# Summing six first-layer tiles of the last chunk in narrower column strips

## The chip, the cores and the metric

The kernel runs on one core of a Trainium2 chip. The metric is the device time of one execution in microseconds (us). Three executions of the kernel before took 631.61, 632.38 and 633.06 us, so its time is the median, 632.38 us. A further execution was recorded by the hardware profiler, and every duration below is read from that recording.

The profile's names for the engines are: PE is the matrix engine, PEld its loads of stationary operands (weights), DVE the vector engine, ACT the scalar engine, POOL the general-purpose engine and SP the engine that issues the transfers (DMA).

## The reference, cut to what matters

The program is an attention layer (local window plus block summaries) followed by two matrix products with a piecewise function between them. Only the second half is touched by the change:

```python
h = x @ w_in                      # x: 3072 x 512, w_in: 512 x 2048
neg = h <= -1.0
pos = h >= 1.0
g = np.where(pos, h, np.where(neg, 0.0, (h + 1.0) ** 2 / 4.0))
out = g @ w_out                   # w_out: 2048 x 512
```

Here `x` is the output of the attention, 4 x 768 tokens of 512 features.

## The kernel before

The 3072 tokens are worked through in eight chunks of 384 (`NCH` = 8, `T` = 384). A chunk c runs through the attention, whose result is written, transposed, into four pairs of tiles `xhi`, `xlo` (`xs[c, k]`, k = 0 to 3, 128 features by 384 tokens each), and then through the two layers.

Every float32 factor of the two layers is kept as a rounded part and a rest, both of the type float32r, and each product is made as three: weight rest times high, weight high times rest, and high times high. The weights (`halves`) are converted once, in the opening, and stay on the chip.

**The first layer**, `ff1` (line 422), makes one tile of `h` for each f = 0 to 15: 128 columns of `w_in` by the chunk's 384 tokens, summed over k = 0 to 3. That is 4 x 3 = 12 matmuls into one PSUM bank, each with a 128 x 128 block of weights as the stationary operand and 384 columns moving (line 426). The first of the twelve has `start`, the last has `stop`. A bank holds 512 columns; `h` uses 384 of them, and two banks take turns (`ps_h`, two buffers).

**The gate** turns `h` into `ghi` and `glo` in five steps on other engines: half (ACT, line 439), square (ACT, 442), minimum (DVE, 445, the last reader of `h`), rounding (ACT, 450), rest (POOL, 455).

**The second layer**, `ff2` (line 457), takes tile f of the gate's output as stationary and 512 columns of `w_out` as moving operand: 3 row blocks x 3 products = 9 matmuls with 512 columns each (line 464), summed over all f into three banks `acc`.

The order of the instructions on each engine is written out by hand as a text of steps: `OPENING` for chunk 0, `SECOND` for chunk 1, `LATER` for the rest. A step is a letter and its arguments: `F.d2` is `ff1` of the present chunk for f = 13 and k = 2, `B.b` is `ff2` for f = 11, `G`, `H`, `I`, `J`, `O` are the five gate steps. In `LATER` the four steps of a tile stand side by side, and the second layer follows two tiles behind:

```python
F.c0 F.c1 F.c2 F.c3 J.b O.b t+32 t+33 B.a G.c H.c u*0 F.d0 F.d1
F.d2 F.d3 I.c z*0 J.c u*1 O.c B.b G.d H.d z*1 I.d F.e0 ...
```

So on PE the last chunk (c = 7, which has no later chunk's attention beside it) is a plain alternation: twelve matmuls of tile f, nine of tile f - 2, twelve of tile f + 1, and so on.

`idle_products` (line 429, steps `j`) multiplies zeros by zeros, 128 x 128 by 128 columns of plain float32, in the opening while PE has nothing else to do. They matter below because they are the only other matmuls with whole 128 x 128 weights and few moving columns.

Of the kernel before, what the change touches and what calls it, by code (L numbers as in the profile page):

```python
# [19 lines left out]
P = 128  # L20
# [11 lines left out]
NCH = B * NHALF  # L32
NK = DM // P
NF = DFF // P
NTT = T // P
W_BUFS = 3
LAG = 2
E_BUFS = 2
OPENING = """
# [56 lines left out]
def fused_kernel(ctx: ExitStack, tc: tile.TileContext, q2, kT, kwin, vT, vwin, w_in, w_out, mask, ident, out):  # L96
    nc = tc.nc
# [24 lines left out]
    weight, raws, converting, joined, halves = {}, {}, {}, {}, {}  # L122

    def room(i, what, shape, dtype):

        return wpool.tile(shape, dtype, tag=f"w{i}", name=f"{what}{i}")
# [25 lines left out]
    def convert_join(i, n):  # L152
# [7 lines left out]
        else:  # L160
            if i not in converting:
                converting[i] = stage.tile([P, 2 * DM], I32, tag="w", name=f"w{i}", bufs=W_BUFS)
            nc.vector.scalar_tensor_tensor(out=converting[i][:, cols], in0=top[:, cols], scalar=-0x80000000, in1=joined[i, part],  # L163
# [15 lines left out]
    q_ts, k_ts, v_ts, s_pss, es, dens, t_pss, pts, vs_pss, o_pss, xs = ({} for _ in range(11))  # L179

    def input_tile(pool, what, shape, c, p):
        if c == 0 and (what, p) in at_first:
            return at_first[what, p]
        tag, bufs = ("w", W_BUFS) if pool is stage else (what, 2)
        return pool.tile(shape, F32, tag=tag, name=f"{what}{c}_{p}", bufs=bufs)
# [3 lines left out]
    for i, share in enumerate(FIRST):  # L189
        at, at_room = 0, room(NF - 1 - i, "first", [P, 4 * DM], F32)  # L190
# [227 lines left out]

    hs, ts, gs, acc, outs = {}, {}, {}, {}, {}

    def ff1(c, f, k):
        if k == 0:
            hs[c, f] = ps_h.tile([P, 512], F32, tag="h", name=f"h{c}_{f}")
        x_hi, x_lo = xs[c, k]
        for n, (w, x) in enumerate(((1, x_hi), (0, x_lo), (0, x_hi))):
            nc.tensor.matmul(hs[c, f][:, :T], weight["win", f][w][:, k * P:(k + 1) * P], x,  # L426
                             start=(k == 0 and n == 0), stop=(k == NK - 1 and n == 2))
# [39 lines left out]
    def result(c, i):  # L467
        o_sb = stage.tile([P, DM], F32, tag="w", name=f"o{c}_{i}", bufs=W_BUFS)
        if i == 1:
            nc.vector.tensor_copy(out=o_sb, in_=acc[c][i])  # L470
        else:
            nc.scalar.copy(out=o_sb, in_=acc[c][i])
        outs[c, i] = o_sb
# [5 lines left out]
    def load_constants(n):  # L479
# [13 lines left out]
        "p": values_of_two, "u": sum_vals_ahead, "z": turn_sums, "x": spread_sums, "L": low,  # L493
        "a": convert_top, "b": convert_low, "c": convert_join, "d": convert_high, "e": convert_rest,
        "F": ff1, "G": gate_half, "H": gate_square, "I": gate_min, "J": gate_high, "O": gate_rest, "B": ff2, "U": result, "o": store, "j": idle_products,
    }
    done = set()
# [92 lines left out]
```

## Time and profile before

| What | Value |
|---|---|
| median of three executions | 632.38 us |
| the profiled execution's own time | 632.96 us |
| its span, first to last instruction | 631.2 us |
| PE busy | 617.1 us, 98% of the span, 4388 matmuls |
| PEld busy | 550.4 us, 87%, 4388 loads |
| DVE, ACT, POOL busy | 57%, 53%, 41% |
| share of the first layer (line 426) in the chain that ended last | 41% |
| share of the second layer (line 464) in it | 42% |
| mean granted PE clock | 0.990 |

The profiled execution took 1.76 us more than its span, which is what lies before the first and after the last instruction. "Busy" for PE means that some matmul was under way; matmuls overlap, so the distance from the start of one to the start of the next says more than the duration of one. PEld is a row of its own because the weights of one matmul are loaded while the matmul ahead of it still runs.

### The profile page before, as it was taken

What the parts mean: (1) busy time and instruction counts of PE and PEld (TensorE: products, weight loads), DVE (VectorE), ACT (ScalarE), POOL (GpSimd) and SP (SyncE); (2) the same over time, 40 slices, a digit from 0 to 9 for tenths busy, and PEclk for the clock granted to TensorE, in tenths of its full rate; (3) what the DMA queues carried; (4) which work ended last, traced back from release to release, by engine and by line L of the source; (5) the groups of instructions that cost most, each with busy time, mean ns of one, the idle gap of its engine ahead of it and who ended that gap; (6) DMA issues with size and microseconds to landing.
All of it is one profiled execution on the core that took longest, in us unless ns stands there. A gap on an engine that the chain in (4) does not pass through costs nothing.

```text
span 631.2 us, 11762 instructions
## 1 busy us (share of the span) xinstructions
PE 617.1 (98%) x4388; PEld 550.4 (87%) x4388; DVE 357.8 (57%) x822; ACT 336.7 (53%) x877; POOL 259.4 (41%) x272
## 2 busy tenths in 40 slices
PE   8689999999999999999999999999999999999997
PEld 7578888898988989898898989889898988999995
DVE  5879787377836549376643737469363726411111
ACT  2679998454547353463635436373543636343342
POOL 2578999533533333333423434333332333212221
PEclk9879999999999999999999999999999999999999
DMA  8999953181124150251213033162202210010001
GB/s 305 299 309 359 275 178 80 54 247 46 52 64 123 51 158 4 78 182 38 74 38 99 25 103 109 38 196 65 73 1 82 79 38 2 1 50 1 2 0 51
DMA packets 49770, 63.57 MB, mean 101 GB/s; under 512 B 24881, under 2 KB 33329, under 8 KB 49713
## 3 DMA queue, kind: packets, MB, share of 16 engines
q1 hardware_dynamic: 49712, 62.81, 33.5%
q8 instruction: 35, 0.57, 0.4%
q14 instruction: 23, 0.18, 0.1%
HBM read 56.51 MB, written 6.29 MB: 99 GB/s over the span
## 4 chain that ended last, share of the span: by engine, by line
PE 91%; DMA 4%; POOL 2%; DVE 1%; ACT 1%; SPq 0%; issue 0%; POOLq 0%; ACTq 0%
PE acc L464 42%; PE h L426 41%; PE o_ps L415 3%; PE s_ps L360 3%; DMA raw<-in_w_in 2%; DMA raw<-in_w_out 1%; POOL halves L175 1%; PE o_ps L332 1%; PE t_ps L320 1%; DMA first<-in_kT 1%; PE h_idle L434 0%; PE s_ps L286 0%; DVE w L163 0%; POOL e L315 0%; DVE c L158 0%
## 5 line engine op out<-in xcount | busy, mean ns | idle before, releaser
L426 PE MATMUL h<-xhi,halves 128*128 128x384 f32 x1024 | 284.7, 339 | 2.8 <-POOL halves L175 1.8
L464 PE MATMUL acc<-halves,ghi 128*128 128x512 f32 x768 | 240.4, 394 | 0.0
L455 POOL TENSOR_TENSOR glo<-t,ghi 128x384 fp32r<-128x384 f32 x128 | 129.7, 1015 | 263.7 <-ACT ghi L450 186.8
L426 PEld LDWEIGHTS h<-xhi,halves 128*128 128x128 f32 x1024 | 187.3, 188 | 9.4 <-POOL halves L175 2.7
L445 DVE SCALAR_TENSOR_TENSOR t<-h,t 128x384 f32<-128x384 f32 x128 | 70.7, 556 | 205.1 <-ACT t L442 200.4
L426 PE MATMUL h<-xlo,halves 128*128 128x384 f32 x512 | 172.0, 336 | 0.0
L464 PEld LDWEIGHTS acc<-halves,ghi 128*128 128x128 f32 x768 | 144.1, 188 | 27.8
L464 PE MATMUL acc<-halves,glo 128*128 128x512 f32 x384 | 152.4, 397 | 0.0
L439 ACT ACTIVATE t<-h,ones_half 128x384 f32<-128x384 f32 x128 | 74.0, 579 | 131.9 <-PE h L426 122.6
L405 DVE STREAM_TRANSPOSE turned_blocks<-e 32x192 f32<-32x192 f32 x288 | 106.5, 370 | 20.5 <-POOL e L393 16.4
L450 ACT CAST ghi<-t 128x384 fp32r<-128x384 f32 x128 | 65.2, 511 | 96.5 <-DVE t L445 94.8
L426 PEld LDWEIGHTS h<-xlo,halves 128*128 128x128 f32 x512 | 96.3, 188 | 4.9
L464 PEld LDWEIGHTS acc<-halves,glo 128*128 128x128 f32 x384 | 72.1, 188 | 14.5 <-issue 2.1
L381 ACT ACTIVATE e<-e,den 128x120 f32<-128x120 f32 x144 | 55.2, 386 | 26.5 <-DVE den L375 26.5
L442 ACT ACTIVATE t<-t 128x384 f32<-128x384 f32 x128 | 66.6, 522 | 2.9
L393 POOL TENSOR_TENSOR e<-e,den 128x720 f32<-128x720 f32 x24 | 33.4, 1391 | 51.0 <-DVE den L387 23.7
L175 POOL TENSOR_TENSOR halves<-w,halves 128x1024 fp32r<-128x1024 f32 x16 | 38.6, 2412 | 5.4 <-DMA q<-in_q 4.2
L381 ACT ACTIVATION_READ_ACCUMULATOR e<-e,den 128x1 f32 x144 | 27.3, 189 | 0.0
L158 DVE SCALAR_TENSOR_TENSOR c<-raw,c 128x512 int32<-128x512 int32 x32 | 22.0, 690 | 6.3 <-ACT raw L144 3.0
L368 DVE SCALAR_TENSOR_TENSOR e<-s_ps,mask_sb 128x360 f32<-128x360 f32 x48 | 22.4, 523 | 5.6 <-PE s_ps L360 5.6
L304 ACT ACTIVATE e<-e,den 128x120 f32<-128x120 f32 x48 | 18.3, 384 | 10.2 <-DVE den L299 10.2
L150 ACT ACTIVATE c<-raw 128x512 int32<-128x512 uint32 x32 | 19.8, 627 | 5.8 <-DMA raw<-in_w_in 4.8
(77 smaller groups left out, 422.3 us busy)
## 6 DMA issues: line engine op xcount, KB each, us to landing
k<-in_kwin SPq DMA_DIRECT2D x28, 360.0 KB, 4.4
v<-in_vwin SPq DMA_DIRECT2D x30, 288.0 KB, 3.4
raw<-in_w_in SPq DMA_DIRECT2D x16, 512.0 KB, 10.1
raw<-in_w_out SPq DMA_DIRECT2D x16, 512.0 KB, 10.1
out<-o SPq DMA_DIRECT2D x24, 256.0 KB, 2.3
q<-in_q SPq DMA_DIRECT2D x56, 96.0 KB, 4.0
kraw<-in_kT SPq DMA_DIRECT2D x13, 384.0 KB, 4.2
vraw<-in_vT SPq DMA_DIRECT2D x13, 384.0 KB, 5.3
```

Of the source, the lines that this page charges most:

```text
L175: nc.gpsimd.tensor_tensor(out=lo, in0=converting[i].bitcast(F32), in1=hi.bitcast(F32), op=ALU.subtract)
L368: nc.vector.scalar_tensor_tensor(out=es[c, h][:, b, j], in0=s_pss[c, p, j][:, :NT * KA].rearrange("p (t n) -> p t n", n=KA), scalar=1.0 / ...
L381: nc.scalar.activation(out=e, in_=e, func=AF.Exp, bias=dens[c, p][:, 0, j, t:t + 1], scale=1.0, accum_out=dens[c, p][:, 1, j, t:t + 1])
L393: nc.gpsimd.tensor_tensor(out=e, in0=e, in1=den.unsqueeze(2).broadcast_to([P, 2 * NT, KA]), op=ALU.mult)
L405: nc.vector.transpose(out=pt[kb * SB:(kb + 1) * SB, :, qb * SB:(qb + 1) * SB], in_=e[qb * SB:(qb + 1) * SB, :, at:at + SB])
L426: nc.tensor.matmul(hs[c, f][:, :T], weight["win", f][w][:, k * P:(k + 1) * P], x, start=(k == 0 and n == 0), stop=(k == NK - 1 and n == 2))
L439: nc.scalar.activation(out=ts[c, f], in_=hs[c, f][:, :T], func=AF.Relu, bias=ones_half, scale=0.5)
L442: nc.scalar.square(out=ts[c, f], in_=ts[c, f])
L445: nc.vector.scalar_tensor_tensor(out=ts[c, f], in0=hs[c, f][:, :T], scalar=1.0, in1=ts[c, f], op0=ALU.max, op1=ALU.min)
L450: nc.scalar.copy(out=hi, in_=ts[c, f])
L455: nc.gpsimd.tensor_tensor(out=lo, in0=ts[c, f], in1=hi.bitcast(F32), op=ALU.subtract)
L464: nc.tensor.matmul(acc[c][i], a[:, rows], weight["wout", f][w], start=(f == 0 and n == 0), stop=(f == NF - 1 and n == 2))
```

## The change

The six tiles f = 4, 5, 8, 9, 12 and 13 of the last chunk are summed strip by strip: a new table gives the widths, and a new function runs the whole sum over k for the first strip of columns, then for the next. A strip has its own `start` and `stop`. All of it is issued in the step for k = 3; the steps for k = 0 to 2 of these tiles issue nothing. The columns computed, the order of the twelve terms of each sum, the bank and the gate's instructions stay as they are. The other ten tiles of the last chunk, and all other chunks, are not touched.

```diff
+STRIPS = {4: (192, 192), 5: (192, 192), 8: (256, 128), 9: (256, 128), 12: (128, 256), 13: (128, 128, 128)}
...
+    def ff1_in_strips(c, f):
+
+        at = 0
+        for width in STRIPS[f]:
+            cols = slice(at, at + width)
+            at += width
+            for k in range(NK):
+                x_hi, x_lo = xs[c, k]
+                for n, (w, x) in enumerate(((1, x_hi), (0, x_lo), (0, x_hi))):
+                    nc.tensor.matmul(hs[c, f][:, cols], weight["win", f][w][:, k * P:(k + 1) * P], x[:, cols],
+                                     start=(k == 0 and n == 0), stop=(k == NK - 1 and n == 2))
+
     def ff1(c, f, k):
         if k == 0:
             hs[c, f] = ps_h.tile([P, 512], F32, tag="h", name=f"h{c}_{f}")
+        if c == NCH - 1 and f in STRIPS:
+            if k == NK - 1:
+                ff1_in_strips(c, f)
+            return
         x_hi, x_lo = xs[c, k]
```

Each matmul brings a load of its 128 x 128 weights with it, so a strip of the same tile loads the same twelve blocks again. Two strips make 24 pairs of load and matmul where there were 12, three strips make 36: 5 x 12 + 24 = 84 pairs more in all.

The program's order on PE shows it. The names are tile, chunk and f (`h7_5` is tile f = 5 of chunk 7), then what moves and the weights; the last entry is partitions by moving columns. Before, the end of tile 5 and the start of the second layer that follows it:

```order
L426 MATMUL h7_5_6344<-xlo7_2_6133,halves4_727 128x384
L426 MATMUL h7_5_6344<-xhi7_2_6132,halves4_727 128x384
L426 MATMUL h7_5_6344<-xhi7_3_6144,halves4_727 128x384
L426 MATMUL h7_5_6344<-xlo7_3_6145,halves4_727 128x384
L426 MATMUL h7_5_6344<-xhi7_3_6144,halves4_727 128x384
L464 MATMUL acc7_0_6264<-halves4_727,glo7_3_6325 128x512
```

With the change, the same place in tile 5, where its first strip ends and its second begins:

```order
L431 MATMUL h7_5_6356<-xlo7_2_6133,halves4_727 128x192
L431 MATMUL h7_5_6356<-xhi7_2_6132,halves4_727 128x192
L431 MATMUL h7_5_6356<-xhi7_3_6144,halves4_727 128x192
L431 MATMUL h7_5_6356<-xlo7_3_6145,halves4_727 128x192
L431 MATMUL h7_5_6356<-xhi7_3_6144,halves4_727 128x192
L431 MATMUL h7_5_6356<-xhi7_0_5773,halves4_727 128x192
L431 MATMUL h7_5_6356<-xlo7_0_5774,halves4_727 128x192
```

Where the second layer stood next, the sum over k begins anew on the other 192 columns; the second layer's nine follow twelve matmuls later. The same seam in tile 13, with three strips of 128:

```order
L431 MATMUL h7_13_6640<-xhi7_3_6144,halves12_1193 128x128
L431 MATMUL h7_13_6640<-xlo7_3_6145,halves12_1193 128x128
L431 MATMUL h7_13_6640<-xhi7_3_6144,halves12_1193 128x128
L431 MATMUL h7_13_6640<-xhi7_0_5773,halves12_1193 128x128
L431 MATMUL h7_13_6640<-xlo7_0_5774,halves12_1193 128x128
```

Nothing moved past anything else: the order on DVE, ACT, POOL and SP has the same rows as before, and on PE only these six tiles have other rows.

## The prediction

> **What bounds the kernel now.** I read the chain that ended last first, since only what lies on it can move the end. In order of time, its last pieces (start, length, what) are these:
>
> ```profile
> 574.41 2.08 PE acc L464 x9
> 576.49 2.10 PE h L426 x12
> 578.59 2.08 PE acc L464 x9
> ...
> 605.80 2.10 PE h L426 x12
> 607.90 2.08 PE acc L464 x9
> 609.98 2.10 PE h L426 x12
> 612.09 2.08 PE acc L464 x9
> 614.17 2.10 PE h L426 x12
> 616.27 2.08 PE acc L464 x9
> 618.36 2.10 PE h L426 x12
> 620.46 6.18 PE acc L464 x27
> 626.64 0.02 issue
> 626.66 0.58 ACT o L472
> ```
>
> The last chunk is an unbroken alternation on PE, with no other engine in it until the final copy. The tiles follow each other every 4.19 us and the last, f = 15, starts at 618.36, so the rows at 576.49, 605.80 and 609.98 are f = 5, 12 and 13. Twelve first-layer matmuls take 2.10 us, **175 ns** a pair of load and matmul; nine second-layer ones take 2.08 us, **231 ns**. Next I asked whether PE pauses anywhere in that stretch (columns: window, its length, then busy time of the engines, the granted clock, DMA):
>
> ```profile
> core 0: us, PE busy (x) PEld busy (x) DVE busy (x) ACT busy (x) POOL busy (x), PEclk, DMA share, GB/s
> 572.30:618.36 46.06, 46.06 (x233) 41.73 (x232) 6.13 (x11) 17.82 (x34) 11.08 (x11) 1.00 0.00 1
> ```
>
> It doesn't: PE is busy for 46.06 of 46.06 us at full clock, and transfers are absent. So whatever a pair costs more goes straight to the end, unless another engine's slack has to be reckoned with. It is wide. Tile 12 ends as its second-layer neighbour starts, at 607.90, and its gate then runs as follows:
>
> ```profile
> 608.00 0.58 ACT L439 ACTIVATE t<-h,ones_half 128x384 f32<-128x384 f32 x1 [1.84 <-PE h L426]
> ...
> 609.24 0.56 DVE L445 SCALAR_TENSOR_TENSOR t<-h,t 128x384 f32<-128x384 f32 x1 [3.63 <-ACT t L442]
> ...
> 610.42 1.01 POOL L455 TENSOR_TENSOR glo<-t,ghi 128x384 fp32r<-128x384 f32 x1 [3.18 <-ACT ghi L450]
> ```
>
> `glo` is ready at 611.43 and PE first wants it two tiles later, at 616.27, so 4.8 us are spare; the bank is free at 609.80 and wanted by tile 14 at 614.17. Longer tiles only widen both. The change is therefore a pure question of PE: what does a pair with 192, 256 or 128 moving columns cost?
>
> **The price of a pair.** Two things can set it. The first is the streaming of the columns. Through 175 ns at 384 columns and 231 ns at 512 runs a line of 56 ns per 128 columns, which gives 119 ns at 256, 91 ns at 192 and 63 ns at 128. The second is the load of the weights. At 178.7 us a first-layer tile follows other work whose array layout is different, and its first load finds no cover (PE rows, then PEld rows):
>
> ```profile
> 178.72 0.44 PE L426 MATMUL h<-xhi,halves 128*128 128x384 f32 x1
> 178.99 0.34 PE L426 MATMUL h<-xlo,halves 128*128 128x384 f32 x1
> 179.17 0.52 PE L426 MATMUL h<-xhi,halves 128*128 128x384 f32 x2
> ```
>
> ```profile
> 178.71 0.19 PEld L426 LDWEIGHTS h<-xhi,halves 128*128 128x128 f32 x1
> 178.82 0.19 PEld L426 LDWEIGHTS h<-xlo,halves 128*128 128x128 f32 x1
> 179.00 0.36 PEld L426 LDWEIGHTS h<-xhi,halves 128*128 128x128 f32 x2
> ```
>
> Read the starts. Elsewhere a load starts as the matmul ahead starts (178.99 and 179.00 are such a pair): only one set of weights can wait behind the set in use. The first matmul is recorded at 178.72, but the next load starts at 178.82, as the columns of the first begin to stream; and the first matmul's record lasts 0.44 us where its neighbour's lasts 0.34. Both say that an uncovered load costs **0.10 to 0.11 us**, although its own record is 0.19 long. Hence the shortest possible rhythm: the matmul starts, the next load starts, 0.11 us later the next matmul starts, however few columns it has. That is a floor which 384 columns (175 ns) hide and 128 do not. One stretch of the opening shows loads at this rhythm, the products of zeros with 128 columns:
>
> ```profile
> 9.48 3.84 PE L434 MATMUL h_idle<-zeros 128*128 128x128 f32 x32
> ...
> 9.48 3.65 PEld L434 LDWEIGHTS h_idle<-zeros 128*128 128x128 f32 x32 [0.16 <-issue]
> ```
>
> From the first to the last load are 3.65 - 0.19 = 3.46 us for 31 steps, **112 ns** each. These are float32, whose columns may stream more slowly, so 112 ns is an upper bound for the load alone; with the 0.10 to 0.11 us from the other side I take 112 ns as the floor. Its ends are 105 ns (the load alone) and 119 ns (what 256 columns cost, the nearest price above).
>
> **The sum.** Pairs with 256 columns are set by streaming (119 ns), those with 192 and 128 by the floor (112 ns):
>
> - f = 4 and 5: 24 x 112 = 2.69 us for 2.10, +0.59 each, **+1.18**
> - f = 8, 9 and 12: 12 x 119 + 12 x 112 = 2.77 for 2.10, +0.67 each, **+2.02**; whether the wide strip comes first makes no difference, as each strip is twelve equal pairs
> - f = 13: 36 x 112 = 4.03 for 2.10, **+1.93**
>
> Together **+5.1 us**. Nothing covers it, and nothing is removed: the seam between two strips is one more pair of the same kind, since the array layout stays the same, and the second `start` waits for nothing, as the operands were ready before the tile began. With the floor at 105 ns the 120 narrow pairs (48 + 36 + 36) give 0.8 less, at 119 ns 0.8 more: +4.3 to +6.0. On the profiled execution's own 632.96 us this makes 638.1; that execution lay 0.6 above the median of 632.38, so against the median it is **637.5 us**, within 636.7 and 638.4.
>
> **The rivals.**
>
> *The loads run ahead, and only streaming counts.* If two sets of weights could wait, or a load were much shorter than 0.11 us, the floor would vanish and the line gives 2 x (24 x 91 - 2100) + 3 x (12 x 119 + 12 x 63 - 2100) + (36 x 63 - 2100) = 168 + 252 + 168 ns, +0.6 us: **633.0 us**, which is no slowdown that can be measured (the bound is 0.2%, 1.3 us). It decides from a load of 63 ns downward, in tile 13 first. Against it speaks every row above in which a load starts with the matmul ahead of it and never sooner, and the 0.11 us uncovered. Chance 0.06.
>
> The Trainium skill speaks for this rival. "TensorE: Matmul & The Clock Gate", section on weight-path perf modes, says that weights of 128 columns whose type is not FP32 are loaded by a fast path of themselves, measured there at about twice the speed. Taken by its name float32r would qualify, a load would be about 54 ns (an estimate from that page's factor and the 0.11 us here), and this change would cost 0.6 us. The rows decide against it: the float32r load at 178.71 is as long, 0.19, as the float32 loads of the opening, 3.65 us for 32 at 112 ns.
>
> *The clock falls.* In tile 13 the array would stream 53 ns of every 112, less than anywhere else in the chunk, for 4 us. In the opening the clock did fall after thin stretches:
>
> ```profile
> 14.64:18.05 3.41, 3.11 (x56) 2.34 (x57) 3.04 (x6) 0.02 (x1) 0.40 (x2) 1.00 1.07 287
> 18.05:21.47 3.42, 0.98 (x9) 0.79 (x8) 2.06 (x7) 2.06 (x3) 1.03 (x2) 1.00 1.02 370
> 21.47:24.88 3.41, 2.88 (x13) 2.73 (x13) 2.89 (x6) 3.36 (x18) 0.82 (x1) 0.50 1.08 282
> ```
>
> PE was busy for 0.98 of 3.42 us, and the next 3.41 us ran at 0.50; after 3.11 busy of 3.41 the clock held. If the gate counted columns and not matmuls under way, one window at half clock would do 1.7 us less work: 637.5 + 1.7 = **639.2 us**. Tile 13 keeps a matmul under way without a gap, so I give it 0.06.
>
> *Narrow strips run as float32 does.* A float32 product is recorded as two passes: the `j` steps of `OPENING` ask for 56 products of zeros, and the records are 112 (duration least/median/most, then first and last start).
>
> ```profile
> L434 PE MATMUL h_idle<-zeros x112: 273/275/579, 1.0 to 27.9; 128*128 128x128 f32 x112
> L426 PE MATMUL h<-xhi,halves x1024: 333/334/629, 30.3 to 620.1; 128*128 128x384 f32 x171
> ```
>
> Float32r has one record for each product (1024 of 8 chunks x 16 tiles x 4 k x 2), but the trace has it at 384 and 512 columns alone. Were strips under 256 columns to take two passes of 112 ns per 128 columns, a narrow pair would cost 224 (128) or 336 ns (192): 2 x 5.96 + 3 x 2.02 + 5.96 = +23.9 us, **656 us**. Nothing in the rows points to a limit on the width; chance 0.05.
>
> *Sums into the same columns need their distance.* No two matmuls that add into the same columns start less than 0.17 us apart in the rows above. If 175 ns were a floor of the adding, 156 pairs x 175 = 27.3 us stand for 6 x 2.10 = 12.6: +14.7, **647 us**. That 175 and 231 lie on one line with the columns speaks against it; chance 0.04.
>
> That the strips are not made is ruled out by the order on PE. Faster than before would need a strip to stream better than in proportion; no row has that, 0.01.
>
> **How the numbers follow.** The floor by the load has 0.76, the rivals 0.06, 0.06, 0.05 and 0.04, and 0.03 is left for what I don't see. The likeliest case spans 636.7 to 638.4; a median of three can lie 0.7 off (631.61 to 633.06 before), and the fallen clock (639.2) is to be inside, so the range is 635.5 to 640.5, and 0.82 of the chance lies in it. Slower by over 0.2% are all but the first rival and part of the rest: 0.92; within 0.2%: 0.07; faster: 0.01.
>
> **What would show it.** In the changed profile PE stays without a pause, and the chain has 2.69 us for tiles 4 and 5, 2.77 for 8, 9 and 12, and 4.03 for 13, with loads of narrow pairs starting 112 ns apart for 192 and 128 columns alike. Equal distances at 192 and 128 are the mark of the floor; distances of 91 and 63 ns mean that loads run ahead, 175 at all widths the adding, over 200 the second pass, and a clock of 0.50 near the end the gate. The prediction is wrong if the six tiles together add less than 4 or more than 7 us.

## The result, and the profile after

The changed kernel takes 637.89 us, the median of 637.62, 637.89 and 638.36, against 632.38 before: a ratio of **1.0089, with a 95% interval from 1.0066 to 1.0112**, or 5.5 us more (4.2 to 7.1). The profiled execution took 637.62 us with a span of 635.8, 4.7 us over the profiled one before.

The chain that ended last, in order of time (start, length, what), from the kernel with the change. Line 431 is the matmul in strips, 443 the untouched first layer, 481 the second layer:

```profile
571.92 2.66 PE h L431 x24
574.58 2.08 PE acc L481 x9
576.65 2.66 PE h L431 x24
...
589.76 2.73 PE h L431 x24
592.49 2.13 PE acc L481 x9
...
607.85 2.78 PE h L431 x24
610.64 2.06 PE acc L481 x9
612.69 3.97 PE h L431 x36
616.66 2.15 PE acc L481 x9
618.81 2.11 PE h L443 x12
620.92 2.08 PE acc L481 x9
```

Take each tile with the nine matmuls behind it, because a part of the last strip's wait is booked on the first of those nine. Before, that was 2.10 + 2.08 = 4.18 us. Now it is 4.74 for tiles 4 and 5, 4.86 for 8 and 9 (the rows of 9 equal those of 8), 4.84 for 12 and 6.12 for 13: 0.56 + 0.56 + 0.68 + 0.68 + 0.66 + 1.94 = **5.1 us**. All of the added time is in these six places. From the start of tile 4 to the end of the span were 58.9 us and are 63.9; the opening came out 0.4 us shorter in this execution, which is why the two profiled executions differ by less.

The window over the six tiles and some of what follows, with the columns as before:

```profile
core 0: us, PE busy (x) PEld busy (x) DVE busy (x) ACT busy (x) POOL busy (x), PEclk, DMA share, GB/s
571.92:620.92 49.00, 49.00 (x308) 45.14 (x307) 5.58 (x10) 16.58 (x31) 11.09 (x11) 1.00 0.00 1
```

PE never pauses and the clock is at 1.00. What a narrow pair looks like shows in the first matmuls of tile 13 (the timeline of PE, then that of its loads):

```profile
612.53 0.22 PE L431 MATMUL h<-xhi,halves 128*128 128x128 f32 x1
612.59 0.28 PE L431 MATMUL h<-xlo,halves 128*128 128x128 f32 x1
612.70 0.39 PE L431 MATMUL h<-xhi,halves 128*128 128x128 f32 x2
612.92 0.27 PE L431 MATMUL h<-xlo,halves 128*128 128x128 f32 x1
```

```profile
612.53 0.19 PEld L431 LDWEIGHTS h<-xlo,halves 128*128 128x128 f32 x1
612.64 0.30 PEld L431 LDWEIGHTS h<-xhi,halves 128*128 128x128 f32 x2
612.87 0.19 PEld L431 LDWEIGHTS h<-xlo,halves 128*128 128x128 f32 x1
612.98 0.30 PEld L431 LDWEIGHTS h<-xhi,halves 128*128 128x128 f32 x2
```

The first matmul had its weights loaded under a wide one; its record is 0.22 us long, and the next record starts 0.06 us later, as its 128 columns are through. From then on every record is 0.27 to 0.28 long: each matmul now holds the array for some 0.05 us before its weights are there. The loads, each of which starts as the columns of the matmul ahead begin to stream, keep a rhythm of 0.11 us (612.53, 612.64, 612.87 behind a pair, 612.98).

### The profile page after: what moved, and what is told of

The parts are those of the page before. It is cut to its first block, busy times and chain, and to the rows that moved or that the text cites. A ratio compares the mean times of both kernels' runs of the same rounds, so it can differ in the third digit from the quotient of the medians.

```text
span 635.8 us, 11930 instructions
## 1 busy us (share of the span) xinstructions
PE 622.2 (98%) x4472; PEld 555.5 (87%) x4472; DVE 358.3 (56%) x822; ACT 336.6 (53%) x877; POOL 259.4 (41%) x272
## 4 chain that ended last, share of the span: by engine, by line
PE 90%; DMA 4%; POOL 2%; ACT 2%; issue 0%; SPq 0%; DVE 0%; POOLq 0%; ACTq 0%
PE acc L481 41%; PE h L443 38%; PE o_ps L416 3%; PE h L431 3%; PE s_ps L361 3%; DMA raw<-in_w_in 2%; POOL halves L176 2%; DMA k<-in_kwin 1%; DMA first<-in_kT 1%; PE t_ps L321 1%; PE o_ps L333 1%; ACT e L305 1%; PE s_ps L287 0%; ACT c L151 0%; PE h_idle L451 0%
## 5 line engine op out<-in xcount | busy, mean ns | idle before, releaser
L443 PE MATMUL h<-xhi,halves 128*128 128x384 f32 x976 | 271.3, 339 | 2.3 <-POOL halves L176 1.3
L443 PEld LDWEIGHTS h<-xhi,halves 128*128 128x128 f32 x976 | 178.4, 188 | 8.7 <-POOL halves L176 2.3
L443 PE MATMUL h<-xlo,halves 128*128 128x384 f32 x488 | 163.9, 336 | 0.0
L443 PEld LDWEIGHTS h<-xlo,halves 128*128 128x128 f32 x488 | 91.6, 188 | 4.6
```

## The experiments

The theory after the result: a pair of load and matmul costs what its columns take to stream, 119 or 120 ns for 256, but never less than the 112 ns that the load of the next 128 x 128 weights takes, since only one load runs ahead. "Before" in these runs had medians of 632.34 and 632.39 us. A run for which no ratio is given is a single execution, and what is read from it is read in its chain and its windows.

### Other widths

```diff
-STRIPS = {4: (192, 192), 5: (192, 192), 8: (256, 128), 9: (256, 128), 12: (128, 256), 13: (128, 128, 128)}
+STRIPS = {4: (352, 32), 5: (320, 64), 8: (288, 96), 9: (240, 144), 12: (224, 160), 13: (32,) * 12}
```

> The six tiles of the last chunk get other widths: 352+32, 320+64, 288+96, 240+144, 224+160, and 12 x 32 for tile 13. Floor theory (a pair costs 7 + 0.4375 ns per column, but never less than the 112 ns of the next weights' load): 32, 64, 96, 144, 160 and 224 columns all cost 112 ns, 240 lies at the edge with 112, 288 costs 133, 320 costs 147, 352 costs 161. Tiles 4, 5, 8, 9, 12 take 3.28, 3.11, 2.94, 2.69, 2.69 us, tile 13 with 144 pairs 16.1 us; together 18.2 us over before, 650.6 us. Rival, cost by the type's width (strips under 256 columns run at another rate): cost falls with the width below 256 columns, so 32 columns are cheaper than 224. Rival, falling clock: tile 13 streams 21 ns of every 112 for 16 us; if the gate counts columns, the granted clock drops to 0.50 there and pairs of 32 columns reach about 214 ns.

Measured: 660.16 us, so the sum of the theory is 9.6 us short. The chain has the miss in one place, tile 13 and the nine matmuls behind it:

```profile
570.20 3.18 PE h L431 x24
...
594.04 2.64 PE h L431 x24
...
607.15 2.64 PE h L431 x24
609.80 2.09 PE acc L481 x9
611.89 25.51 PE h L431 x144
637.39 3.97 PE acc L481 x9
```

The first five tiles agree with the theory to 0.05 us once the nine matmuls behind each are counted. Across all widths from 32 to 240 the starts of the loads lie 112 ns apart (medians of 111.5 to 112), at 288 columns 131.5, at 320 147 and at 352 161: the cost below 256 columns does not fall with the width, which rules out the rival of another rate for narrow strips. Tile 13 is the rival of the falling clock, as it stood in the prediction, but with 32 columns in place of 128. Windows over its two parts, PE and loads of line 431 alone:

```profile
core 0: us, PE busy (x) PEld busy (x), PEclk, DMA share, GB/s
611.89:617.30 5.41, 5.41 (x51) 5.41 (x50) 1.00 0.00 0
617.30:637.39 20.09, 20.09 (x95) 19.98 (x94) 0.50 0.00 1
```

After 5.4 us of strips of 32 the granted clock halves, and the pairs take 213 ns for 112. That is 9.4 us more in the tile and 1.9 in the nine matmuls behind it; the opening was 2.1 us shorter in this execution, which takes some of it back.

### The same pairs, turn by turn

```diff
+        for k in range(NK):
+            x_hi, x_lo = xs[c, k]
+            for n, (w, x) in enumerate(((1, x_hi), (0, x_lo), (0, x_hi))):
+                for h, cols in tiles:
+                    nc.tensor.matmul(h[:, cols], weight["win", f][w][:, k * P:(k + 1) * P], x[:, cols],
+                                     start=(k == 0 and n == 0), stop=(k == NK - 1 and n == 2))
```

Here `tiles` holds the bank of `h` for the first strip and free banks for the others.

> The widths of the change, but the strips take turns inside each product, so that two or three matmuls in a row have the same weights; the further strips sum into free banks of the attention, and the gate's first and third step read them strip by strip (1 to 2 more instructions each on ACT and DVE, which have 4.8 us to spare). Floor theory (every pair loads its weights, equal or not, one load ahead): the same pairs in another order, 112 ns for narrow ones and 119 for 256 columns, so 637.5 us, the time of the change, within 0.5 us. Rival, equal weights are not loaded again: only the first strip of a product waits for a load; 192+192 costs 91 + 112 in place of 224 ns, 3 x 128 costs 63 + 63 + 112 in place of 336, 256+128 stays; 2 x 0.25 + 1.2 us less, 635.8 us. Rival, sums into the same columns need distance: turns between banks would make the narrow pairs cheaper, down to 91 and 63 ns, 633 us.

Measured: 637.93 us, ratio to before 1.0088 (1.0071 to 1.0104), the time of the change. Tiles 4, 8 and 13 in the chain:

```profile
572.99 2.66 PE h L433 x24
...
590.83 2.72 PE h L433 x24
...
613.78 3.97 PE h L433 x36
```

These are the lengths of the change to 0.01 us, and the trace has as many loads as matmuls, 4472 each. Weights that are already in the array are loaded again, and neither the order nor the bank matters. That rules out the rival of the sums: with turns between banks no two neighbours add into the same columns, and the price stays.

### Shorter loads under the same columns

```diff
+EXTRA = {4: 128, 8: 64, 13: 32}
...
+    def extra(c, f, m):
+
+        spare = ps_att.tile([P, 512], F32, tag="att", name=f"spare{c}_{f}")
+        for at in range(0, T, P):
+            cols = slice(at, at + P)
...
+                    nc.tensor.matmul(spare[:m, cols], weight["win", f][w][:, k * P:k * P + m], x[:, cols],
```

> The kernel before, with 36 products more of 128 moving columns in each of the tiles 4, 8 and 13 of the last chunk, summed into a free bank that nobody reads: with 128 columns of weights in tile 4, 64 in tile 8, 32 in tile 13. The 128 moving columns are the same in all three. Floor theory (the load sets it): 112 ns a pair in tile 4, 36 x 112 = 4.0 us; with 64 and 32 columns of weights the load is about a half and a quarter, the streaming of 63 ns sets the pace, 36 x 63 = 2.3 us each and 0.1 us for each change of the array's layout; together 8.9 us, 641.3 us. Rival, a matmul of this type costs at least as much as 256 columns (or 112 ns by itself) whatever its weights: 4.0 us in all three, 644.5 us.

Measured: 641.65 us (theory 641.3, rival 644.5). The three stretches with 128, 64 and 32 columns of weights, in the chain:

```profile
574.66 3.97 PE spare L430 x36
...
595.42 2.16 PE spare L430 x36
...
618.55 2.16 PE spare L430 x36
```

With the same 128 moving columns, halving the weights takes a pair from 3.97 / 36 = 0.110 us to 2.16 / 36 = 0.060; halving them again changes nothing, since now the streaming sets the pace. So the floor belongs to the load and not to the streaming of the columns. Fewer columns of weights also mean fewer rows of sums to write; the run with other types, below, separates the two.

### All sixteen tiles of the last chunk

```diff
+STRIPS = {f: (128, 128, 128) for f in range(NF)}
```

> All sixteen tiles of the last chunk in 3 x 128. Floor theory: 16 x (36 x 112 - 2100) ns = +30.9 us on before, 663.3 us; PE stays without a pause and the clock at 1.00. Rival, falling clock: over 97 us PE streams 53 ns of every 112 in two thirds of the time; each window of 3.41 us at half clock adds up to 1.7 us, so some windows of 0.50 and 665 us or more. Rival, slack of the gate: none is lost, tiles grow longer, so the gate's outputs are ready earlier against their use; PE would show waits if this were wrong.

Measured: 662.59 us, ratio 1.0480 (1.0462 to 1.0497), 30.3 us over before where 30.9 were expected. A window that holds the sixteen tiles (554.59 to 650.22 in the chain, each 3.97 us) and the 6 us before them:

```profile
548.60:650.00 101.40, 101.40 (x740) 94.66 (x739) 10.34 (x19) 27.39 (x52) 17.09 (x17) 1.00 0.03 9
```

The price adds up tile by tile and no other engine comes into it. The clock stays at 1.00 throughout; as the nine matmuls of the second layer stand between the tiles, this does not yet show what a long unbroken stretch of 128 columns does.

### The same strips in chunk 3

```diff
-        if c == NCH - 1 and f in STRIPS:
+        if c == 3 and f in STRIPS:
```

> The six tiles with the same strips, in chunk 3 in place of the last one; there the attention of the next chunk stands between the tiles on PE and keeps ACT, DVE and POOL busier. Floor theory: PE has no pause there either, so the price is the same, +5.1 us, 637.4 us. Rival: if another engine paces chunk 3, PE has slack there and a part of the 5.1 us is hidden, down to 632.3 us.

Measured: 637.34 us, ratio 1.0078 (1.0051 to 1.0105), 5.0 us more. The last chunk is no special place: PE sets the pace in chunk 3 as well. The interval of the times (3.2 to 6.6 us) would leave room for a part that is hidden, but the chain of this run has the six tiles at 2.66, 2.66, 2.73, 2.73, 2.78 and 3.97 us, the lengths of the change, with PE alone in it there.

### Long stretches of narrow pairs

```diff
+EXTRA = {4: 128, 8: 96, 12: 64}
...
+    def extra(c, f, width):
+
+        spare = ps_att.tile([P, 512], F32, tag="att", name=f"spare{c}_{f}")
+        for _ in range(10):
...
+                    nc.tensor.matmul(spare[:, :width], weight["win", f][w][:, k * P:(k + 1) * P], x[:, :width],
```

> The kernel before, with 120 pairs more in each of the tiles 4, 8 and 12 of the last chunk, summed into a free bank that nobody reads: 128 moving columns in tile 4, 96 in tile 8, 64 in tile 12, each with whole 128 x 128 weights. Floor theory with the clock at 1.00: 120 x 112 = 13.4 us each whatever the width, 40.3 us, 672.6 us. What the clock does tells two readings of the run with 12 x 32 apart, where it fell to 0.50 after 5.4 us. If it counts the columns that stream, a share of 53/112 at 128 columns holds (sixteen tiles of 3 x 128 did, though with the second layer between), 27/112 at 64 columns falls, and 96 columns (40/112) lie in between and are open. If it falls on any stretch of narrow pairs that is long enough, all three fall. A stretch that falls goes on at about 213 ns a pair, some 7 us more for it and up to 4 us more in what follows.

Measured: 694.83 us, 22.2 us above the sum at full clock. Windows over the stretch of 128 columns, the two parts of that of 96, and the two parts of that of 64 (PE and loads of this line alone):

```profile
573.51:586.86 13.35, 13.35 (x120) 13.21 (x119) 1.00 0.01 1
603.64:607.20 3.56, 3.56 (x34) 3.56 (x34) 1.00 0.00 0
607.20:625.75 18.55, 18.55 (x88) 18.39 (x87) 0.50 0.00 1
645.09:648.20 3.11, 3.11 (x30) 3.11 (x30) 1.00 0.00 0
648.20:667.60 19.40, 19.40 (x92) 19.27 (x91) 0.50 0.00 1
```

128 columns hold the clock for 13 us, 96 and 64 lose it after 3 to 4 us, although PE is as "busy" in all three: 13.35 of 13.35, 22.11 of 22.11. The three stretches have the same 120 pairs, 112 ns apart while the clock is full, and differ in the moving columns alone. So neither the length of the stretch nor the time in which a matmul is under way decides, but how much streams in that time; the limit lies between 96 and 128 columns for every 112 ns. Whether the gate counts columns or something that goes with them is not shown. The clock stayed at 0.50 for 23.9 us each time, some 5 us beyond the end of the stretch.

### Other types

```diff
+EXTRA = {4: "bf16", 12: "f32"}
...
+                    if kind == "bf16":
+                        half = zeros.bitcast(mybir.dt.bfloat16)
+                        nc.tensor.matmul(spare[:, :P], half[:, :P], half[:, P:2 * P], start=(k == 0 and n == 0), stop=(k == NK - 1 and n == 2))
+                    else:
+                        nc.tensor.matmul(spare[:, :P], zeros, zeros, start=(k == 0 and n == 0), stop=(k == NK - 1 and n == 2))
```

> The kernel before, with 120 products of zeros, 128 x 128 by 128 columns, in each of two tiles of the last chunk, summed into a free bank that nobody reads: in tile 4 as bfloat16, in tile 12 as float32. Floor theory: float32 has two passes for each product, each with its own load of 112 ns, 240 x 112 = 26.9 us, as in the opening; for bfloat16 the load decides, and if it is about half as long as that of the wide types, as the Trainium skill has it (TensorE: Matmul & The Clock Gate, section on weight-path perf modes), pairs take 56 to 63 ns, 7 us for 120. Rival, the floor belongs to the matmul and not to the load: bfloat16 at 112 ns as well, 13.4 us. Together 666 us, or 673 us by the rival.

Measured: 664.92 us. The two stretches in the chain, bfloat16 and float32:

```profile
572.81 6.71 PE spare L431 x120
...
613.06 26.80 PE spare L433 x240
```

A pair of bfloat16 costs 6.71 / 120 = 56 ns, one pass of float32 26.80 / 240 = 112 ns, with the same 128 x 128 weights and the same 128 columns. The records of the loads are 98 ns long for bfloat16 and 192 for float32, as they are for float32r in the change. The bfloat16 matmuls write as many rows of sums as those of the change and still come every 56 ns, so the floor of 112 is not in the writing of the sums. The price of float32 doesn't show the load by itself: there the record of a matmul starts together with a load (both at 619.82), as it does in the wide tiles, where the streaming sets the pace, and not 0.05 us ahead of one as in tile 13. By these records the columns of a float32 pass take about as long as its load, some 0.11 us. The Trainium skill ("TensorE: Matmul & The Clock Gate", section on weight-path perf modes) has weights of 128 columns loaded by a fast path unless their type is FP32. For bfloat16 the trace agrees (a load in at most 56 ns); the loads of float32r, with records of 192 ns and a floor of 112, are as slow as those of FP32.

## Why the prediction was right, point by point

**The bound.** The chain of the last chunk was PE alone, and the added work went to the end in full: 5.1 us in the six tiles. The slack of the gate played no part; in the run with sixteen tiles, too, the chain is PE alone.

**The price of a pair.** The floor of 112 ns came out as 112 ns at 128 and at 192 columns, the sign named in the prediction. It rested on the uncovered load at 178.71 and on the products of zeros, and each could have meant something else. The products of zeros did: in the opening, too, their records start together with a load (both at 9.81), so their 112 ns can be the time of their own columns. That this equals the floor of float32r is luck; the sound witness was the uncovered load of 0.10 to 0.11 us. The run with shorter loads settles it: at equal columns, the length of the load decides, and the bfloat16 pairs of 56 ns show that it is not the rows written. The 119 ns for 256 columns came out as 120; the straight line through 384 and 512 columns held within 2 ns down to 256.

**The sum.** Predicted and found: 0.59 and 0.56 for tiles 4 and 5, 0.67 and 0.68 for 8 and 9, 0.67 and 0.66 for 12, 1.93 and 1.94 for 13. The forecast was 637.5 us and 637.89 were measured, a distance that lies within the spread of the executions (637.62 to 638.36). Strip order within a tile made no difference, as expected.

**The rivals.** That loads run ahead is ruled out by the change itself: 5.1 us in the six tiles, where this rival had 0.6. That they are skipped for equal weights is ruled out turn by turn (637.93 us). That narrow strips take a second pass (224 ns and more a pair) is ruled out by 112 ns from 32 to 240 columns and by one load for each product: 4472 loads, the 4388 of before and the 84 added. That sums need a distance of 175 ns is ruled out by the 112, and that turns between banks would make them cheaper by the run that took such turns.

**One reason was wrong.** Against the falling clock the prediction set that tile 13 "keeps a matmul under way without a gap". That isn't what the gate looks at: strips of 96, 64 and 32 columns have no gap either and lose the clock. The forecast stood because 128 columns lie on the safe side of the limit (13.35 us of them without a break kept 1.00), which no row shown of the kernel before tells; in this the prediction was lucky. The price given for it, 1.7 us for one window, was too low for a stretch that goes on: 22.1 us in place of 13.4 at 96 columns, and 1.9 us more in the nine matmuls behind.

## What to carry to other kernels

A float32r matmul with 128 x 128 weights costs about 7 ns + 0.44 ns for each moving column, but at least 112 ns, the load of the next weights (measured at full clock, from 32 to 512 columns); so keep strips at 256 columns or more, and price a split by counting the loads that it adds, whether or not the weights are the same. To price an operation that the trace lacks, look for a place where its usual cover is missing: one uncovered load gave this floor to about 0.01 us. Where narrow matmuls run for several us, read the granted clock and not the busy time, since PE can look fully busy and still fall to half its clock.

## What the runs showed of the hardware that was not expected

The clock of PE fell to 0.50 in the middle of unbroken work: 5.4 us into strips of 32 columns, 3.6 us into strips of 96, 3.1 us into strips of 64, and not with strips of 128, either in 13.35 us without a break or in sixteen tiles of them with the second layer between. The Trainium skill ("TensorE: Matmul & The Clock Gate", Part 1) names an idle window of about 3.4 us as the cause of the lower clock; here no window was idle by the profile, while the length of the window agrees: 23.9 us are seven times 3.41, and the two falls of one execution, at 607.2 and 648.2, lie 41.0 us apart, twelve times 3.41. So the times fit a fixed grid of 3.41 us. Each fall ends the first step of the grid that the narrow pairs fill (at 64 columns all but 0.3 us of it), and each return ends the first step that is free of them. The 5.4, 3.6 and 3.1 us are then only the place of the start in the grid, and the seven steps come from the length of the stretch.

The recorded start of a matmul that waits for its weights isn't the start of its columns: in tile 13 the records start as the matmul ahead is through, and the 0.05 us of waiting lie inside the record of the matmul that waits. The starts of the loads give the true rhythm.
